# Backward row pairs, per-head global keys and an earlier hand-over of PSUM banks in a fused attention, Fourier mixing and FFN kernel

## The chip, the cores and the metric

The kernel runs on one core of one Trainium2 chip. The metric is the device time of one execution in microseconds (us); lower is better. TensorE is called PE, its weight loads PEld, VectorE DVE, ScalarE ACT, GpSimd POOL and SyncE SP.

## The reference

Attention over 768 positions in 4 batches and 8 heads of 64, with a local window of 96, 8 global keys and a linear bias by distance; then a two-dimensional Fourier transform of the attention's result (its real part is added to it), a normalisation, and an FFN with ReLU of width 2048:

```python
def _attn_ref(q, k, v, n_global, n_local):
    scores = scale * np.matmul(q, k.transpose(0, 1, 3, 2))
    is_global = pos[None, :] < int(n_global)                 # 8
    is_local = (rel >= 0) & (rel < int(n_local))             # 96
    dist = np.where(is_global & ~is_local, float(n_local), np.abs(rel))
    scores = scores - slopes[:, None, None] * dist
    scores = np.where(is_global | is_local, scores, -1e9)
    a = softmax(scores)
    return np.matmul(a, v)

def _moe_ref(x, w_ch1, w_ch2):
    mixed = np.real(np.fft.fft(np.fft.fft(x, axis=1), axis=2))
    u = x + mixed
    un = (u - mean(u)) / np.sqrt(var(u) + 1e-6)
    return u + np.maximum(un @ w_ch1, 0.0) @ w_ch2
```

Here `x` is the attention's result, [4, 768, 512]. q, k, v, the FFN's two matrices and the result are float32 in HBM; the products are made in float16.

## The kernel before, in words

A batch's work is done by head pairs (`hp`, four of them). A pair's q and k are loaded as float16, transposed into `qkT` (`trans`: on PE for batches 0 and 1, by a transposing DMA on SP for batches 2 and 3), multiplied in three groups of 128-row tiles (`score`; in batches 0 and 1 the bias is added by products of `sid` and `dist`), and exponentiated on ACT into `ex`. The global keys are treated apart. `kg_copies` picks the first eight keys of each head into `kG`, `glob` multiplies them with q into a [64, 512] tile whose rows are (pair, head, key), one exp on ACT makes `EG` from it, and `v_global` picks the eight value rows with a selection matrix `sel` on PE; their copies in PSUM go to `vG` on ACT or DVE. `ones` makes the column of ones in `vG` in the same way at the start. `av` multiplies `ex` with the values and adds the global part, 130 columns for both heads of a pair in one product. A norm on DVE divides into `x`.

The Fourier part folds `x` on DVE (`fold_0`, `fold_s`, `fold_d`), multiplies the folded parts with a table of cosines and sines along the positions (`y_unit`, four groups), and multiplies the results with a second table along the features (`u_unit`). The 768 positions are 6m + r with m = 0 to 127 and r = 0 to 5; rows are the six values of r, and PAIRS says which two are made together: (1, 2), (0, 3), (4, 5). Since the transform of a real input is symmetric, not all of its parts are multiplied: rows 4 and 5 are read from parts of rows 2 and 1 that POOL has reversed (`mirror`, line 962). In batch 0 `x` is added on PE by products with a 0-1 matrix (`spread`, line 993); in the others `x` is written to HBM (`bounce`, `xd`), read back in the order of rows (`xr`), and added on DVE (line 1039).

`nt_unit` transposes the normalised rows, `ph_unit` makes the FFN's first products (eight groups for each pair of rows, counted by c = 3b + pair), `pg_unit` the second ones, and the last four row pairs use a form with fewer products (`pg_units`, `pgA` and `pgD`). Stores to HBM go by SP.

The order of each engine's instructions is made before the program runs: a planner (class `Plan`) keeps a clock for every engine, takes from four lists (MIX, ATT, PH, PG, looking ten units ahead in the first two) what it thinks can start first, and corrects these times by a table BIAS. Its costs (`act`, `dve`, `pl.pe(...)`, `dma=`) are estimates written in the code. PSUM has eight banks: ring `xx` has two slots of two banks, `C` and `D` are two banks each for the attention of the first batches, and are given back together (token `("CD",)`), when all their users are done, as the rings `ph` and `pg`. Every buffer is counted, so a unit waits until the buffer that it overwrites is free.

Loads with a cast go by POOL's software queue, in the order in which they're listed. At the start SP loads the first pair's q and k as float32 (they're cast on ACT or DVE), then `ident`, `dist` and `gb`; meanwhile PE runs 12 products of zeros (`pz`, line 1384).

Of the kernel before, what the change touches and what calls it, by code (L numbers as in the profile page):

```python
# [9 lines left out]
FP16 = mybir.dt.float16  # L10
# [12 lines left out]
class Plan:  # L23
# [8 lines left out]
    LAND = {}  # L32
    LAT = {"ACT": 0.14, "DVE": 0.12, "POOL": 0.08}

    def __init__(self):
        self.t = {"PE": 0.0, "ACT": 0.0, "DVE": 0.0, "POOL": 0.0, "SP": 0.7, "DMA": 3.75, "DMA2": 1.9}
        self.tok = {}
        self.ready = []
        self.pending = []
        self.rings = {}  # L40
        self.left = {}
        self.n = 0
        self.lanes = [0.0] * 8
        self.soft = [0.0] * 8
# [64 lines left out]
    def emit(self, place):  # L109
# [8 lines left out]
        if dma:  # L118
            q = "DMA2" if outs and outs[0] in (("ld", 0), ("ld", 1), ("c", "id"), ("c", "dist"), ("c", "gb")) else "DMA"
            end = self.t[q] = max(self.t[q], end) + dma  # L120
        else:
            lat += self.LAT.get(eng, 0.0)
# [26 lines left out]
    def slot(self, tag):  # L149
# [7 lines left out]
    BIAS = {('mk1', '*', 4): 1.5, ('y', 1, 2, 2, 'r'): -3, ('qk', '*', 2): -0.7, (2, 90): -0.7, ('ob', '*', 2): -0.3,  # L157
            (3, '*', 7): -1.5, ('ex', 2, 2, 0): 1.5, ('ss', '*', 6): 0.3, (0, 20): -3, (1, 57): -0.7, ('mk1', '*', 5): 1.5,
            ('v', '*', 1): 1.5, ('c', 't2'): -0.3, ('mk1', '*', 7): 0.7, ('kG', '*', 1): 0.7, ('z', 1, 0): 3, ('u', 2, 0): 0.7}
# [4 lines left out]
    AQ = (4, 5)  # L164
    ORD = {("qk", 0): 0, ("v", 0): 0, ("qk", 1): 5, "w1": 6, "gate": 7, ("v", 1): 8, "w2": 9, ("qk", 2): 10, ("v", 2): 10, ("qk", 3): 10, ("v", 3): 10}

    def run(self, streams):

        left = [[(*u, (i, k)) for k, u in enumerate(s)] for i, (s, _) in enumerate(streams)]
        while True:  # L170
            best = None
            for i, s in enumerate(left):
                for k, (needs, ring, _, name) in enumerate(s[:self.LOOK if streams[i][1] else 1]):
# [3 lines left out]
                    if ring is not None:  # L177

                        there = [(min(self.rings[g])[0], g) for g in ring
                                 if self.rings[g] and not (g in ("C", "D") and ("CD",) in self.tok)]  # L180
# [27 lines left out]
def act(n):  # L208
    return 0.06 + n / 1200.0


def dve(n):
    return 0.085 + n / 960.0
# [11 lines left out]
def kernel(  # L225
# [63 lines left out]
    sel = np.zeros((P, 128))  # L289
    gpos = np.flatnonzero(tau < NG)  # L290
    for h in range(4):
        for g in range(NG):
            sel[gpos[g], h * 32 + h * NG + g] = 1.0
    gb = np.zeros((64, 1))
    for h in range(H):
        at = 32 * (h // 2 % 2) + 16 * (h // 4) + 8 * (h % 2)
        gb[at:at + NG, 0] = -slopes[h] * NL
    perm = np.zeros((P, 9, 64))
    for rho in range(3):
        for jj in range(3):  # L300
            for m in range(64):
                y = 3 * m + rho - 64 * jj
                if 0 <= y < 64:
                    perm[y, 3 * rho + jj, m] = perm[64 + y, 3 * rho + jj, m] = 1.0
    ident_sel = np.concatenate([np.eye(P), sel], 1)
# [20 lines left out]
    early = {"ctx": tc.tile_pool(name="pse", bufs=1, space=bass.MemoryType.PSUM)}  # L326
    early["pool"] = early["ctx"].__enter__()

    def bank(tag, name, dtype=FP32):
        if tag in ("C", "D"):  # L330
            return early["pool"].tile([P, 2, 512 if dtype == FP32 else 1024], dtype, tag=tag, name=name, bufs=1)
        if tag == "xx":
            return ps.tile([P, 2, 512 if dtype == FP32 else 1024], dtype, tag=f"{tag}{tag.k}", name=name, bufs=1)
        if "late" not in early:
            early["ctx"].__exit__(None, None, None)
            early["late"] = ctx.enter_context(tc.tile_pool(name="psl", bufs=1, space=bass.MemoryType.PSUM))
        return early["late"].tile([P, 512], FP32, tag=f"{tag}{tag.k}", name=name, bufs=1)

# [12 lines left out]
    ident = kon.tile([P, 256], FP16, tag="ident", name="ident")  # L351
    sel_sb = ident[:, 128:256]
# [4 lines left out]
    gb_sb = kon.tile([64, 1], FP32, tag="gb", name="gb")  # L357
# [7 lines left out]
    one = kon.tile([P, 1], FP16, tag="one", name="one")  # L365
# [3 lines left out]
    vG = [kon.tile([P, H, 66], FP16, tag=f"vG{i}", name=f"vG{i}") for i in range(2)]  # L369

    EG = kon.tile([P, 512], FP16, tag="eg", name="eg")
# [32 lines left out]
    def load_qk(b, hp):  # L404
# [3 lines left out]
        for w, src in enumerate((q, k)):  # L408
# [14 lines left out]
            if n == 0:  # L423
                def read(w=w, rows=rows):
                    t = stage["u", w] = buf("u", w, [P, 2 * NP, 2 * Dh], FP32, 1)
                    nc.sync.dma_start(t, rows)
                pl.later([("SP", 0.45, read)], [], 0.0, [("ld", w)], lat=1.7, dma=1.35)

                def cast(on, w=w):
                    place()  # L430
                    copy_on(on, qk16[n][:, w].rearrange("p h n t d -> p (h n) (t d)"), stage["u", w])
                pl.later([("ACT", act(768), lambda cast=cast: cast("ACT")), ("DVE", dve(768), lambda cast=cast: cast("DVE"))], [("ld", w)], 0.0,
                         [("qk", 0, w)], [("free", "u", w)], rank=0)
# [19 lines left out]
    pl.users(("CD",), 4 * HP + 4 + HP + len(YG) + NP + 1)  # L453

    def BANKS(b):
        return ("xx", "C", "D") if b < pl.CDB else ("xx",)

    def CD(b, ring):
        if b == 1 and ring in ("C", "D"):
            pl.left[("CD",)][0] += 1  # L460
            return [("CD",)]
        return [("CD",)] if b == 0 else []
# [5 lines left out]
    def kg_copies(b, hp):  # L468
        n = HP * b + hp
        for s in range(2):  # L470
            def cp(on, s=s):
                c0 = 16 * (hp // 2) + 8 * s
                on.tensor_copy(  # L473
                    kG[b % 2][64 * s:64 * s + 64, hp, c0:c0 + NG].rearrange("p (t m) -> p t m", t=2),
                    TT[n][64 * s:64 * s + 64, 1, 0:P].rearrange("p (t m) -> p t m", t=2)[:, :, 0:NG // 2])
            pl.later([("POOL", 0.2, lambda cp=cp: cp(nc.gpsimd))] + [("DVE", 0.12, lambda cp=cp: cp(V))] * (b == 0), [("qkT", n)] + ([("gldone", b - 2, hp % 2)] if b > 1 else []), 0.0,
# [1082 lines left out]
```

## Time and profile before

| | us |
|---|---|
| runs (median of 3, lowest, highest) | 262.46, 262.13, 262.70 |
| the profiled execution | 262.43 |
| its span, first to last instruction | 260.5 |
| busy: PE, PEld, DVE, ACT, POOL | 246.3, 178.8, 163.1, 142.9, 120.6 |
| FFN: ph (768 products), pg (256 products) | 93.3, 61.1 |
| spread L993 (36), second transform L1017 (192 in three forms) | 4.6, 8.5 + 4.4 + 2.2 |
| av L685 (352), with the global part L677 (64) | 16.9, 12.6 |
| first transposition, first ph | starts at 8.29, 50.62 |
| end of the last product, end of the span | 257.1, 260.5 |

A busy time is the time in which at least one instruction of the group was under way; PE's instructions overlap, so the mean duration of one is longer than the distance between two. Times within the profile count from the span's start. The granted clock of PE is given in tenths of full speed by slice; over the span it is 0.993.

### The profile page before, as it was taken

Reading aid. Unit: us, or ns where it says so; the run is one execution under the profiler, and the core shown is the slowest. Engines: PE = TensorE matmul, PEld = TensorE weight load, DVE = VectorE, ACT = ScalarE, POOL = GpSimd, SP = SyncE. Lnnn points to the kernel's source line nnn. Section 1 sums busy time; section 2 is a strip of 40 time slices with the busy share of each in tenths; the row PEclk is TensorE's granted clock in tenths of the full one; section 3 lists DMA queues with packets and bytes.
Section 4 is the critical chain, followed back from the end, with each engine's and each line's share of the span. In section 5 each row is a group of like instructions: output and inputs, shape, how many; then the busy total and the mean of one; then the engine's idle time right before and its main releaser. Section 6 shows DMA issues by size and latency. Waiting matters only on the chain.

```text
span 260.5 us, 6774 instructions
## 1 busy us (share of the span) xinstructions
PE 246.3 (95%) x2824; PEld 178.8 (69%) x2824; DVE 163.1 (63%) x362; ACT 142.9 (55%) x240; POOL 120.6 (46%) x212
## 2 busy tenths in 40 slices
PE   7798789899979999999999999999999999999994
PEld 2566545589748676575477466588779578888883
DVE  1549996537982746712277987778996555625463
ACT  4198798685636698851055743884645236533300
POOL 8798876724938988999921304030304011010000
PEclk9799999999999999999999999999999999999999
DMA  7999999997999999999968941401450540300222
GB/s 175 174 165 179 274 207 108 90 194 102 138 159 218 158 138 149 140 112 123 114 126 167 178 182 48 115 3 43 108 178 0 83 121 0 93 30 3 81 83 81
DMA packets 93630, 31.52 MB, mean 121 GB/s; under 512 B 81664, under 2 KB 89984, under 8 KB 93600
## 3 DMA queue, kind: packets, MB, share of 16 engines
q0 software_dynamic: 66096, 14.18, 62.5%
q1 hardware_dynamic: 24672, 12.19, 21.2%
q10 hardware_dynamic: 2832, 4.72, 6.9%
q8 instruction: 22, 0.36, 0.6%
q14 instruction: 8, 0.07, 0.1%
HBM read 30.95 MB, written 8.65 MB: 152 GB/s over the span
## 4 chain that ended last, share of the span: by engine, by line
PE 55%; POOL 19%; DMA 17%; ACT 3%; DVE 3%; issue 2%; ACTq 0%; POOLq 0%
PE ph L1144 18%; PE pg L1168 12%; POOL qk L414 10%; DMA v<-in_v_dram 7%; DMA qk<-in_q_dram 6%; PE pgD L1249 5%; POOL v L400 5%; DMA w<-in_moe_w_ch_dram 4%; PE pgA L1249 4%; PE pav L685 3%; PE py L914 3%; PE pu L1017 2%; PE pt L507 1%; DVE x L704 1%; POOL hT L438 1%
## 5 line engine op out<-in xcount | busy, mean ns | idle before, releaser
L1144 PE MATMUL ph<-unT,w 128*128 128x256 f16 x768 | 93.3, 273 | 2.9 <-ACT hT L1150 1.7
L1144 PEld LDWEIGHTS <-w 128*128 128x128 f16 x768 | 73.1, 98 | 16.1 <-issue 4.9
L1150 ACT ACTIVATE hT<-ph 128x512 f16<-128x512 f32 x83 | 48.9, 596 | 47.6 <-PE ph L1144 47.3
L1168 PE MATMUL pg<-w,hT 128*128 128x512 f16 x256 | 61.1, 379 | 0.0
L1168 PEld LDWEIGHTS <-hT 128*128 128x128 f16 x256 | 24.1, 98 | 23.8 <-issue 1.2
L1089 POOL TENSOR_SCALAR sm<-sm 128x2 f32<-128x2 f32 x12 | 3.0, 254 | 57.4 <-ACT un L1082 57.2
L400 POOL DMA_DIRECT2D v<-in_v_dram x32 | 24.7, 823 | 0.7 <-DMA hT<-in_k_dram 0.7
L583 ACT ACTIVATE ex<-sc 128x992 f16<-128x992 f32 (+2 forms) x24 | 20.6, 928 | 7.1 <-DVE qkT L514 5.6
L580 ACT ACTIVATE er<-sc 128x768 f16<-128x768 f32 (+2 forms) x24 | 21.6, 925 | 4.5 <-PE sc L555 3.3
L414 POOL DMA_DIRECT2D qk<-in_k_dram x32 | 21.4, 750 | 4.6 <-DMA qk<-in_k_dram 3.1
L1177 DVE SCALAR_TENSOR_TENSOR u<-pg,sm,u 128x512 f32<-128x512 f32 x16 | 12.0, 750 | 18.0 <-PE pg L1168 18.0
L414 POOL DMA_DIRECT2D qk<-in_q_dram x32 | 21.4, 730 | 3.4 <-DMA qk<-in_q_dram 2.0
L1073 ACT ACTIVATE un<-u,sm 128x512 f16<-128x512 f32 x17 | 11.8, 717 | 19.1 <-DVE sm L1043 17.6
L962 POOL COPY ww<-zy 128x512 f16<-128x512 f16 x16 | 10.1, 661 | 21.4 <-PE py L914 14.4
L595 DVE TENSOR_TENSOR ex<-er,mk 128x768 f16<-128x768 f16 (+2 forms) x24 | 15.4, 662 | 4.2 <-ACT er L580 4.2
L1082 ACT ACTIVATE un<-un 128x512 f16<-128x512 f16 x24 | 14.9, 625 | 4.5 <-DMA unT<-un 4.5
L1039 DVE SCALAR_TENSOR_TENSOR u<-pu,xr 128x512 f32<-128x512 f32 x18 | 11.7, 688 | 9.0 <-PE pu L1017 9.0
L685 PE MATMUL pav<-v,ex 128*128 128x65 f16 x352 | 16.9, 193 | 0.0
L473 POOL COPY kG<-qkT 64x8 f16<-64x8 f16 x28 | 9.6, 342 | 15.7 <-DMA qkT<-qk 12.8
L685 PEld LDWEIGHTS <-ex 128*128 128x128 f16 x352 | 15.6, 97 | 0.8 <-issue 0.2
L1151 DVE TENSOR_SCALAR hT<-ph 128x512 f16<-128x512 f32 x13 | 9.0, 690 | 8.3 <-PE ph L1144 8.3
L931 DVE CAST zy<-py 128x512 f16<-128x512 f32 (+1 forms) x8 | 7.1, 892 | 10.4 <-PE py L914 8.2
(143 smaller groups left out, 388.6 us busy)
## 6 DMA issues: line engine op xcount, KB each, us to landing
out_dram<-u SPq DMA_DIRECT2D x23, 256.0 KB, 2.1
w<-in_moe_w_ch_dram POOLq DMA_DIRECT2D x8, 512.0 KB, 11.0
v<-in_v_dram POOLq DMA_DIRECT2D x32, 96.0 KB, 6.5
xr<-xd ACTq DMA_DIRECT2D x3, 768.0 KB, 4.7
qk<-in_q_dram POOLq DMA_DIRECT2D x32, 48.0 KB, 4.0
qk<-in_k_dram POOLq DMA_DIRECT2D x32, 48.0 KB, 3.7
xd<-x ACTq DMA_DIRECT2D x4, 384.0 KB, 4.6
hT<-in_q_dram POOLq DMA_DIRECT2D x5, 192.0 KB, 7.4
```

The costliest lines, as they stand in the source:

```text
L400: nc.gpsimd.dma_start(v16[b % 2][64 * t:64 * t + 64, h0:h0 + 2, :, 0:Dh].rearrange("m h i d -> m (h i) d"), v[b, h0:h0 + 2].rearrange("h ( ...
L414: nc.gpsimd.dma_start(qk16[n][64 * t:64 * t + 64, w, :, h], src[b, h0 + h].rearrange("(i m t) d -> t m i d", m=64, t=2)[t])
L580: A(mine(), cut(pa), AF.Exp, 0.0, 0.125)
L583: A(cut(expst[hp][:, :, g * 512:g * 512 + (384 if g == 2 else 512)]), cut(pa), AF.Exp, 0.0, 0.125)
L595: VT(o, mine(), m, op=ALU.mult)
L685: nc.tensor.matmul(o[:, s * 65:(s + 1) * 65], lhsT, v16[b % 2][:, 2 * hp + s, i, 0:65], start=(j < 2 and a == 0), stop=(a == len(ops) - 1) ...
L1082: A(x, x, AF.Square, accum_out=MV[c][:, a, 2:3])
L1144: nc.tensor.matmul(ph[:, a * CH:(a + 1) * CH].rearrange("p (x m) -> p x m", x=2), W1[0][:, d, jb * P:(jb + 1) * P], UNT[c][:, :, d, :], st ...
L1150: pl.later([("ACT", act(512), lambda: A(dst, ph, AF.Relu)), ("DVE", dve(512), lambda: V.tensor_scalar_max(dst, ph, 0.0))], [], e, [("h", c ...
L1168: nc.tensor.matmul(pg, HT[c][:, jb, t * P:(t + 1) * P], W2[0][:, jb, :], start=(jb == 0), stop=(jb == NJ - 1))
L1177: V.scalar_tensor_tensor(UT[c][:, t, :], pg, MV[c][:, t, 3:4], UT[c][:, t, :], op0=ALU.mult, op1=ALU.add)
L1249: nc.tensor.matmul(o, lhs(j), rhs(j), start=(first and j == 0), stop=(j == NK - 1), skip_group_check=True)
```

## The change

The parts, as the code does them:

1. `ident` is loaded first on SP, then the first pair's q; its k and `dist` are loaded by ACT. q is cast on DVE, k on ACT. 18 instead of 12 products of zeros.
2. Batch 0's order is pair 0's scores, pair 2's transposition, the global keys of pairs 0 and 2, pair 1's transposition, pair 2's scores, av of pair 0, and so on. Before the first score group of each batch-0 pair, four products of `ident` with `dist` are put into the same bank and overwritten.
3. Global keys: each pair has its own 32 rows (eight keys used, the rest with a bias of -30000), each head its own half of `EG`; glob's products use one head's 64 rows each, two exps take the place of one. The value rows come from HBM by 16 small SP loads and are copied on ACT or DVE. `sel`, `ones` and `v_global`'s products are gone. av's global part is two products of 65 columns.
4. Rows 4 and 5 are rows 2 and 1 backwards: in batches 1 to 3 the same bank of rows 1, 2 is evacuated a second time in reverse (`back`), and rows 4 and 5 have no products of their own; partition p then holds m = 127 - p, so `xr`'s rows 4, 5 are gathered and the result is scattered by indirect DMA on POOL, with a list of row numbers `back_sb`. In batch 0 the products are made, from unreversed parts, with the spread reversed. `mirror` keeps only its first copy. PAIRS is (1, 2), (4, 5), (0, 3).
5. spread reads `x` in its own order and writes PSUM with a step.
6. Banks C and D have tokens of their own: C goes to `ph`, D to `pg`. y groups 2, 3 and the later u units of batch 0 use only `xx` and `D`. The units of rows 1, 2 come after y groups 0 and 1.
7. The read-back of `xd` is issued by SP.
8. The planner's costs, landing times and BIAS are other numbers.

```diff
-    LAND = {}
+    LAND = {("c", "id"): 3.0, ("ld", 0): 4.8, ("ld", 1): 5.0, ("c", "dist"): 6.3, ("c", "gb"): 6.5}
...
+    BIAS = {('h', 7, 2): 1.5, ('g0', '*', 1): 1.5, ('ss', '*', 7): 1.5, ('rd', '*', 10): -0.3, ('u', 3, 0): 1.5, (1, 19): 0.3,
...
+    HW = (0,)
+    U0 = 2
+    PZ = 18
+    FILL = 4
+    EARLY = ("qk2", "qk1", "v0", "v2", "qk3", "v1", "v3")
...
+                    (nc.scalar if w else nc.sync).dma_start(t, rows)
...
+            for _ in range(pl.FILL if b == 0 and g == 0 else 0):
+                nc.tensor.matmul(pa[:, 0, :], idn, dist_sb[:, 0, 0:512], start=True, stop=True, skip_group_check=True)
...
-            e = pl.pe(0.25 + 0.21 * pem, start, True)
+            e = pl.pe(0.27 + 0.28 * pem, start, True)
...
+    def v_global(b):
+        for hp in range(HP):
+            r = slice(32 * HQ[hp], 32 * HQ[hp] + NG)
+            def ld(hp=hp, r=r):
+                nc.sync.dma_start(vgs[r], v[b, 2 * hp:2 * hp + 2, 0:NG, :].rearrange("h g d -> g h d"))
+            def cp(on, hp=hp, r=r):
+                dst = vG[b % len(vG)][r, hp, :, 0:Dh]
...
+            for n in ns:
+                for s in range(2):
+                    r, o = slice(64 * s, 64 * s + 64), 32 * HQ[n % HP]
+                    nc.tensor.matmul(pg[o:o + 32, s, :], kG[b % 2][r, n % HP, :],
+                                     TT[n][r, 0, 256:S], start=True, stop=True, tile_position=(64 * s, o))
...
+                for s in range(2):
+                    A(EG[rows, s], pg[rows, s, :], AF.Exp, gb_sb[rows, s:s + 1], 0.125)
...
-                        nc.tensor.matmul(o.rearrange("p (h d) -> p h d", d=65), EG[:, (j - 2) * P:(j - 1) * P], vG[b % 2][:, 2 * hp:2 * hp + 2, 0:65],
-                                         start=True, stop=False, skip_group_check=True)
                     for s in range(2):
+                        if j >= 2:
+                            nc.tensor.matmul(o[:, s * 65:(s + 1) * 65], EG[:, s, (j - 2) * P:(j - 1) * P], vG[b % len(vG)][:, hp, s, 0:65],
+                                             start=True, stop=False, skip_group_check=True)
...
-            eng.dma_start(XR[b], rows)
+            nc.sync.dma_start(XR[b][:, 0:4], rows[:, 0:4])
+        def rg():
+            nc.gpsimd.indirect_dma_start(out=XR[b][:, 4:6].rearrange("p r d -> p (r d)"), out_offset=None,
+                                         in_=XD[b].rearrange("(n r) d -> n (r d)", r=2),
+                                         in_offset=bass.IndirectOffsetOnAxis(ap=back_sb[:, 0:1], axis=0))
...
-    PAIRS = ((1, 2), (0, 3), (4, 5))
+    PAIRS = ((1, 2), (4, 5), (0, 3))
...
-                        nc.tensor.matmul(pu[64 * h:64 * h + 64, a, :].rearrange("p (r n) -> p r n", r=4), PX[0][t, 3 * (r // 2) + jj],
-                                         X[0][t, 3 * h + jj].rearrange("p (n r) -> p r n", r=4), start=(jj == 0), stop=False,
+                        hx = 1 - h if pr == 1 else h
+                        nc.tensor.matmul(pu[64 * h:64 * h + 64, a, :].rearrange("p (r n) -> p n r", r=4), PX[0][t, 3 * (r // 2) + jj],
+                                         X[0][t, 3 * hx + jj].rearrange("p (n r) -> p n r", r=4), start=(jj == 0), stop=False,
...
+                evac(c, pu, ring, e, pr)
+                if pr == 0:
+                    evac(c + 1, pu, ring, e, 1)
...
+        def back():
+            fresh(c)
+            u, sm = UT[c], MV[c]
             for a in range(2):
+                o, x = (t[:, i].rearrange("p (n r) -> p r n", r=4) for t, i in ((u, a), (XR[b], 4 + a)))
+                i = pu[:, 1 - a, ::-1].rearrange("p (r n) -> p r n", r=4)
+                V.scalar_tensor_tensor(o[:, 1:4], i[:, 0:3], 1.0, x[:, 1:4],
+                                       op0=ALU.mult, op1=ALU.add, accum_out=sm[:, a, 0:1])
+                V.scalar_tensor_tensor(o[:, 0, 1:P], i[:, 3, 0:P - 1], 1.0, x[:, 0, 1:P],
+                                       op0=ALU.mult, op1=ALU.add, accum_out=sm[:, a, 4:5])
+                V.tensor_tensor(u[:, a, 0:1], pu[:, 1 - a, 0:1], XR[b][:, 4 + a, 0:1], op=ALU.add)
...
-        needs = [("unT", c), ("w1", jp // 2)] + (free("hT", 4 + c) if jp == 0 else []) + [("CD",)]
+        needs = [("unT", c), ("w1", jp // 2)] + (free("hT", 4 + c) if jp == 0 else []) + [("C",)]
...
+    def store_back(c, needs):
+        b = c // NP
+        def st():
+            nc.gpsimd.indirect_dma_start(out=out.rearrange("b (n r) d -> (b n) (r d)", r=2),
+                                         out_offset=bass.IndirectOffsetOnAxis(ap=back_sb[:, b:b + 1], axis=0),
+                                         in_=UT[c].rearrange("p r d -> p (r d)"), in_offset=None)
...
-        needs = [("h", c, 2 * part), ("h", c, 2 * part + 1), ("w2", part)]
+        needs = [("h", c, 2 * part), ("h", c, 2 * part + 1), ("w2", part), ("D",)]
```

## The prediction

> **What bounds the kernel now.** I read the page first: engines' busy time, then the span in slices.
>
> ```profile
> span 260.5 us, 6774 instructions
> ...
> PE 246.3 (95%) x2824; PEld 178.8 (69%) x2824; DVE 163.1 (63%) x362; ACT 142.9 (55%) x240; POOL 120.6 (46%) x212
> ...
> PE   7798789899979999999999999999999999999994
> ...
> PEclk9799999999999999999999999999999999999999
> ```
>
> TensorE is the bound, and the page has no other engine near it. From slice 13 on it stands at 9. What can be gained is either less TensorE work, or the holes of the first 12 slices. So next the table by stage, cut where the first transposition, the first FFN product and the last product stand.
>
> ```profile
> 0.00:8.30 8.30, 5.01 (x22) 1.77 (x22) 1.36 (x12) 2.97 (x3) 7.26 (x17) 1.00 0.88 179
> 8.30:50.60 42.30, 37.10 (x745) 24.99 (x741) 32.10 (x102) 32.02 (x47) 33.24 (x55) 0.96 1.59 170
> 50.60:128.00 77.40, 75.29 (x797) 53.36 (x798) 39.97 (x76) 46.72 (x83) 60.00 (x97) 1.00 1.52 149
> 128.00:200.00 72.00, 71.80 (x777) 51.85 (x774) 57.77 (x117) 41.66 (x70) 16.03 (x37) 1.00 0.46 105
> 200.00:257.10 57.10, 57.07 (x496) 46.87 (x494) 31.37 (x59) 19.55 (x38) 4.05 (x11) 1.00 0.21 58
> ```
>
> The columns are stage, length, busy PE, PEld, DVE, ACT, POOL, clock, DMA. A busy PE isn't a PE at its pace, so I priced each stage's products by the spacing of their starts in the timeline where they run packed: ph 0.109 us (8 in 0.87), pg 0.2155, pu L1017 0.056 (16 in 0.89), av 0.030 for 65 columns and 0.056 for 130, a batch-0 or -1 score group some 0.4, twelve L993 products 1.46. The four stages from 8.3 hold 31.6, 72.7, 70.0 and 56.5 us of work in 42.3, 77.4, 72.0 and 57.1 us. Lost: 10.7, 4.7, 2.0 and 0.6. Two thirds of the loss lies before the first FFN product. The start, from the timeline of PE:
>
> ```profile
> 1.17 4.80 PE L1384 MATMUL pz<-eg 128*128 128x512 f16 x12 [1.17 <-DVE eg L1379]
> 8.10 0.27 PE L1423 MATMUL pones<-one,ident 128*32 128x1 f16 x8 [2.12 <-DMA ident<-idm]
> 8.29 2.87 PE L507 MATMUL pt<-ident,hT 128*64 128x128 f16 x48
> ...
> 17.91 0.86 PE L507 MATMUL pt<-ident,hT 128*64 128x128 f16 x24
> ```
>
> The warm-up ends at 5.97, PE idles until ident lands, and the 48 transpositions then take 2.87 us where 24 later take 0.86: the clock of 5 to 15 us is granted at 0.88 and 0.78. The one long hole later is told by the timeline of all engines:
>
> ```profile
> 75.74 0.35 ACTq L732 DMA_DIRECT2D xr<-xd  x1
> 76.14 0.74 ACT L1407 ACTIVATE mk<-distk 128x640 f16<-128x640 f16 x1 [4.01 <-DMA xd<-hT]
> ...
> 77.41 1.91 PE L1144 MATMUL ph<-unT,w 128*128 128x256 f16 x16 [1.74 <-ACT hT L1150]
> ```
>
> ScalarE's queue stood 4.0 us at the read-back of xd, waiting for the write; the ReLU behind it came late, and PE idled 1.74 us.
>
> **The change part by part.** The sum is against the profiled execution, 262.43 us (span 260.5 and 1.9 around it); the median of the runs is 262.46.
>
> *First pair and warm-up: -1.1.* Before, q landed about 3.96 and k about 5.77 (the casts L443 start there), ident at 8.1. Ident now leaves first on SP, k on ScalarE. Even if q and k land no earlier than 5.8, the two casts of 0.84 lie side by side and end by 6.6. The warm-up of 18 products ends later: the first ten step by 0.43 us, to about 5.5, the other eight by 0.2155, so 7.2. Transpositions start at 7.2 instead of 8.3. The six products more cost nothing while the casts last, and 0.6 beyond.
>
> *The clock of the first products: -1.8.* 48 transpositions at the later pace are 1.7 instead of 2.87, and the six following blocks of scores lose some 0.6 less. Four filler products before each batch-0 pair's first scores are 4 x 4 x 0.2155 = 3.4 us. They run while VectorE copies qkT (0.96 us, L514), which the scores need. For the first pair all four are covered; for the others partly. If no cover were left they would cost 3.4, with full cover nothing; I charge 1.4.
>
> *The rest of the stage 8.3 to 50.6: -2.5.* The order is now pair 0's scores before pair 2's transposition, and av of pair 0 before pair 1's scores. ScalarE's first exp came at 12.18; from 7.2 it is 0.9 transposition, 1.0 copy, 0.3 scores: 9.4. VectorE sat idle 2.24 us before 18.81, then ran full to 39.3: its first norm can now lie some 4 us earlier, in that idle time. But ScalarE has two eg exps more of 0.68 in batch 0, and pair 3's load still comes by the same gpsimd queue (pt at 17.91), so I count 2 us of the 3 to 4, not all. Products for rows 1, 2 now follow y groups 0 and 1 with no reversed copy, and ph needs only bank C: the first ph, at 50.6 before, comes near 44, and ph products fill holes that attention left. After clock and start the stage had 8.9 us of loss; I take 4 of it away and charge those 1.4 of filler, rounding -2.6 to -2.5 and not charging the filler twice.
>
> *Row pairs 4, 5 in batches 1 to 3: -2.7.* 48 products of L1017 at 0.056 go. POOL loses L962 (10.1 us) and half its kG copies (9.6). VectorE's backwards evacuation: two of 384 at 0.55 (0.687 less 128 columns of 1.05 ns, the slope between L1267's 256 and 512), two of 127 at 0.28, accumulator reads of 0.08, five small ones of some 0.16: 2.8 instead of 1.7, so +1.1 three times. VectorE is at 63%; this is covered as long as the PSUM slot isn't wanted. It is held 4.5 us instead of 1.7. I charge 0.5 in all.
>
> *Global keys: -1.1.* 32 value selections (0.03 each) and eight ones-products go, 1.2. Their eight copies give way to sixteen of 128 columns on eight partitions (0.2 to 0.25) behind small SP loads. 64 av products of 130 columns become 128 of 65: two times 0.030 against 0.056, +0.3. The 16 glob products become 32 on half the rows; pairs of these can overlap. If they don't, +3.4; if four overlap as L559's four tiles do, -1; I take -0.2. ScalarE gets five more exps of 0.68, three of them in stages with 40% idle.
>
> *Read-back moved to SP: -1.7.* The 4.0 us wait is then SP's. Behind it stand batch 2's transpositions by DMA, issued from 78.3 and used for scores after 94: covered. In batches 1 to 3 rows 4, 5 of xr come by a gather on POOL, 0.75 to 0.85 us by the nearest rows (L400, L414), after xr has landed at 80.4, 152 and 195; 4 us later they are there, by 84.5, 156.5 and 199.5. The first evacuations ran at 86.35, 158.76 and 200.01. Two fit, the third fits because rows 1, 2 go first. Four scattered stores replace eight SP stores; POOL's loads wait behind one of them until its rows are ready.
>
> [...] No row of this trace has an indirect transfer. [...]
>
> *The spread L993: 0, with both ends kept.* Twelve now take 1.46 with a strided moving operand, against 0.65 for three rounds of four tiles. The change reads contiguously and writes PSUM in strides. [...] The trace has no strided PSUM write, so I leave the row's time.
>
> Sum: -1.1 -1.8 -2.5 -2.7 +0.5 -1.1 -1.7 = -10.4. The new order of everything else, which the planner derives from changed costs and biases, isn't seen; later stages hold 7.3 us of loss, 1.7 already spent, so it can give little and can cost. I charge 1. 262.4 - 9.4 = **253.0 us**.
>
> **The rivals.** *(a) Half of it, 256 to 260, chance 0.20.* Batch 0 is held by loads: av waits for v (a wait at 15.9 shows it), pair 3 lands at 17.9 whatever was done at the start, and fillers and the two exps take what is freed. Then only the 7 or so us of removed work and stall, less the order's costs, remain: 257. For it: ScalarE is full from 12.2 to 20, VectorE from 19 to 39. Against it: their first idle ends 3 us sooner.
>
> *(b) Slower, 266, chance 0.15.* [...]
>
> *(c) The steps do as told, 249 to 256, chance 0.62.* *(d) Nothing to see, 0.03*: filler and order cancel it.
>
> **How the numbers follow.** The likeliest is (c), 253.0. 248.5 is this with the spread's gain of 2.4 and an order that costs nothing and hides the filler. Upwards the range takes all of (a) and, to 261.5, the part of it where glob does not overlap or the spread is slower, leaving out (b) and a few in 100 below. A difference under 0.2% (0.5 us) can't be told from none. Faster: (c), (a): 0.82; same 0.03; slower 0.15.
>
> **What would show it.** First transposition near 7.2 at full clock; first ph near 44; no wait of ScalarE for xd; POOL's indirect DMAs near 1 us; 144 instead of 192 L1017 products; L993's twelve near 1.5; VectorE's backwards part near 2.8. Wrong would be PE holes behind pu's slot, POOL busy above 130 us, or the stage from the first ph on longer than its work by more than the present 7 us.

## The result, and the profile after

The change makes the kernel 0.7% faster: the ratio to the kernel before, measured side by side, is **0.9931 [0.9903, 0.9959]**, about 1.8 us of 262.8. Medians of all twenty runs are 261.34 us after (258.81 to 266.68) and 262.76 us before. The forecast was 253.0, so the direction held, at the upper end of the range, and the size was a fifth of it.

The profiled execution of the changed kernel took 264.43 us and is one of four slow ones that the ratio leaves out, so the profile of the experiment e7 stands beside it: the same kernel but for the queue that issues one kind of transfer, with a span of 258.2 us and a full clock (1.00) in every window that is read here.

The page of the changed kernel:

```profile
span 262.7 us, 6833 instructions
...
PE 246.2 (94%) x2838; PEld 177.1 (67%) x2838; DVE 165.4 (63%) x399; ACT 145.0 (55%) x243; POOL 116.0 (44%) x185
...
PE   7888989999999999997995899999999999999994
...
PEclk9999999999999999999999599999999999999999
```

A slice is 6.57 us. Up to slice 6 (39 us) the digits sum to 48 tenths against 46 before, and a part of these is filler; slices 7 to 12, now all at 9, have gained. The clock is now full in every slice up to there. A new hole stands at slice 22 (138 to 145 us), and in the next one the clock falls to half. The stages, cut at the first transposition, the first ph and the last product, with the columns of the table of before (length, PE, PEld, DVE, ACT, POOL, clock, DMA):

```profile
0.00:6.80 6.80, 5.35 (x20) 2.04 (x20) 3.38 (x25) 2.12 (x2) 6.19 (x14) 1.00 0.79 191
6.80:49.60 42.80, 37.66 (x793) 25.39 (x792) 30.48 (x95) 33.77 (x48) 29.50 (x44) 1.00 1.67 181
49.60:128.00 78.40, 75.97 (x797) 52.97 (x784) 41.96 (x94) 48.90 (x89) 62.77 (x100) 1.00 1.49 145
128.00:200.00 72.00, 67.99 (x732) 47.45 (x731) 55.38 (x118) 36.99 (x63) 10.09 (x16) 0.95 0.50 102
200.00:259.30 59.30, 59.28 (x520) 49.26 (x518) 33.71 (x69) 23.20 (x44) 7.42 (x13) 1.00 0.19 57
```

The stage up to the first ph was to shrink from 42.3 to about 37 us. It is 42.8 us long. Pricing the products again by the spacing of their starts (one set of prices for all three kernels, so that the figures for before differ by up to 0.6 from the prediction's), work and lost time in us are:

| stage | before: work, lost | changed, as profiled | changed, e7's profile |
|---|---|---|---|
| first transposition to first ph | 31.2, 11.2 | 34.3, 8.6 | 34.4, 7.8 |
| first ph to 128 | 72.9, 4.5 | 73.3, 5.1 | 72.2, 5.7 |
| 128 to 200 | 69.7, 2.3 | 63.6, 8.4 | 69.3, 2.7 |
| 200 to the last product | 56.7, 0.4 | 58.9, 0.4 | 54.5, 0.3 |

In the first row the lost time did fall by about 3 us, and the work rose by as much: 16 filler products of 0.2155 are 3.4 us. TensorE's holes were filled with filler. The third row shows what this one execution lost beyond e7's, 5.7 us; no part of the account below rests on it. PE's timeline of the changed kernel:

```profile
1.45 5.40 PE L1428 MATMUL pz<-eg 128*128 128x512 f16 x18 [1.45 <-DVE eg L1423]
6.78 0.86 PE L527 MATMUL pt<-ident,hT 128*64 128x128 f16 x24
7.57 1.04 PE L555 MATMUL sc<-dist,ident 128*128 128x512 f16 x4
...
38.81 1.03 PE L933 MATMUL py<-t,ww 128*128 128x256 f16 x8
...
49.66 0.50 PE L1178 MATMUL ph<-unT,w 128*128 128x256 f16 x3
...
124.23 0.28 PE L1023 MATMUL pu<-t,rev 128*128 128x128 f16 x2 [1.81 <-POOL rev L969]
126.12 0.40 PE L650 MATMUL pgl<-qkT,kG 64*32 64x512 f16 x6 [0.62 <-POOL kG L494]
145.25 0.59 PE L577 MATMUL sc<-qkT 64*128 64x256 f16 x4 [3.92 <-DMA qkT<-qk]
```

The abbreviations are the kernel's names: pt transpositions, sc scores, py and pu the two steps of the Fourier part, pgl the global keys. The first transposition is at 6.78 (8.29 before) and the first 24 take 0.86, the full pace. But y starts at 38.81 (before 38.99), and the first ph at 49.66 (before 50.62). 1.5 us won at the start are 0.2 us thirty microseconds later. Then come three waits, for POOL's reversed copy, for its kG copy, and for the transposing DMAs of batch 3; for the same things the kernel before waits 0.2 us at most. In e7 they are 1.7, 0.6 and 1.2 us.

### The profile page after: what moved, and what is told of

It reads as the page before. It is cut to its first block, busy times and chain, and to the rows that moved or that the text cites. A ratio compares the mean times of both kernels' runs of the same rounds, so it can differ in the third digit from the quotient of the medians.

```text
span 262.7 us, 6833 instructions
## 1 busy us (share of the span) xinstructions
PE 246.2 (94%) x2838; PEld 177.1 (67%) x2838; DVE 165.4 (63%) x399; ACT 145.0 (55%) x243; POOL 116.0 (44%) x185
## 4 chain that ended last, share of the span: by engine, by line
PE 51%; DMA 18%; POOL 18%; ACT 5%; issue 3%; SPq 1%; DVE 1%; POOLq 0%; ACTq 0%
PE ph L1178 18%; PE pg L1211 11%; POOL qk L433 10%; DMA qk<-in_k_dram 8%; PE pgD L1295 5%; DMA w<-in_moe_w_ch_dram 5%; PE pgA L1295 4%; POOL v L419 4%; DMA hT<-in_k_dram 3%; DMA qkT<-qk 3%; PE py L933 2%; ACT ex L605 2%; PE pav L695 2%; SPq L505 1%; PE pu L1023 1%
## 5 line engine op out<-in xcount | busy, mean ns | idle before, releaser
L1184 ACT ACTIVATE hT<-ph 128x512 f16<-128x512 f32 x85 | 50.2, 597 | 54.5 <-PE ph L1178 54.1
L1211 PEld LDWEIGHTS <-hT 128*128 128x128 f16 x256 | 24.4, 98 | 24.7 <-issue 1.7
L602 ACT ACTIVATE er<-sc 128x992 f16<-128x992 f32 (+2 forms) x24 | 21.7, 924 | 9.5 <-PE sc L577 6.3
L419 POOL DMA_DIRECT2D v<-in_v_dram x32 | 26.0, 863 | 0.9 <-DMA hT<-in_k_dram 0.6
L433 POOL DMA_DIRECT2D qk<-in_q_dram x32 | 22.1, 778 | 3.3 <-DMA qk<-in_k_dram 2.3
L617 DVE TENSOR_TENSOR ex<-er,mk 128x992 f16<-128x992 f16 (+2 forms) x24 | 14.8, 629 | 13.4 <-ACT er L602 13.2
L433 POOL DMA_DIRECT2D qk<-in_k_dram x32 | 22.2, 825 | 0.9 <-DMA v<-in_v_dram 0.9
L1195 POOL DMA_INDIRECT out_dram<-u,back x4 | 4.6, 1142 | 39.3 <-DVE u L1313 21.0
L1108 ACT ACTIVATE un<-u,sm 128x512 f16<-128x512 f32 x12 | 8.6, 721 | 12.1 <-DVE sm L1090 7.4
L688 PE MATMUL pav<-vG,eg 128*128 128x65 f16 x128 | 14.3, 193 | 0.9 <-DVE x L714 0.9
L948 ACT ACTIVATE zy<-py 128x1024 f16<-128x1024 f32 (+1 forms) x14 | 11.3, 841 | 6.1 <-PE py L933 5.6
L1295 PEld LDWEIGHTS <-hT 128*128 128x128 f16 x128 | 12.5, 98 | 1.8
L714 DVE TENSOR_TENSOR x<-pav,rc 128x384 f16<-128x384 f32 x24 | 12.6, 554 | 0.6
```

The source lines that it names most:

```text
L419: nc.gpsimd.dma_start(v16[b % 2][64 * t:64 * t + 64, h0:h0 + 2, :, 0:Dh].rearrange("m h i d -> m (h i) d"), v[b, h0:h0 + 2].rearrange("h ( ...
L433: nc.gpsimd.dma_start(qk16[n][64 * t:64 * t + 64, w, :, h], src[b, h0 + h].rearrange("(i m t) d -> t m i d", m=64, t=2)[t])
L602: A(mine(), cut(pa), AF.Exp, 0.0, 0.125)
L617: VT(o, mine(), m, op=ALU.mult)
L688: nc.tensor.matmul(o[:, s * 65:(s + 1) * 65], EG[:, s, (j - 2) * P:(j - 1) * P], vG[b % len(vG)][:, hp, s, 0:65], start=True, stop=False, ...
L1184: pl.later([("ACT", act(512), lambda: A(dst, ph, AF.Relu)), ("DVE", dve(512), lambda: V.tensor_scalar_max(dst, ph, 0.0))], [], e, [("h", c ...
```

## The experiments

**e1, no fillers.** `FILL = 0` in place of 4.

> The sixteen filler products are left out; order and all else are as after the change. Theory A (the stage before the first FFN product is held by VectorE, ScalarE and the loads, and the fillers fill holes of PE): no change within 0.3%, first ph within 0.5 us of 49.7. Rival (the fillers are work that the stage pays for, since three of the four pairs' keys lie transposed before): the ratio to the kernel before falls by 0.006 to 0.013, first ph 2 to 3.5 us earlier. If the fillers hold the clock up, the granted clock between 7 and 20 us falls instead and the time rises by 1 us or more.

Measured: ratio 0.9813 [0.9758, 0.9869], which does not overlap the interval of the changed kernel. The difference of 0.0118 is 3.1 us; both intervals together leave 1.5 to 4.7. PE's timeline without fillers:

```profile
6.92 0.86 PE L527 MATMUL pt<-ident,hT 128*64 128x128 f16 x24
...
8.83 0.41 PE L581 MATMUL sc<-qkT 64*64 64x256 f16 x8 [0.72 <-DVE qkT L534]
...
37.40 1.03 PE L933 MATMUL py<-t,ww 128*128 128x256 f16 x8
...
48.25 1.92 PE L1178 MATMUL ph<-unT,w 128*128 128x256 f16 x16
```

The cover that the prediction named is there: PE waits 0.72 us for the qkT copy when no filler stands in it. Four fillers last 0.96 us (7.57 to 8.54 in the timeline of the changed kernel), so the four groups are work of 3.4 to 3.8 us. Yet y and the first ph come only 1.4 us earlier without them (1.8 against e7's first ph). About half of the filler was covered, and loads are a part of the cover: in e1 PE waits 2.7 us for later q and k loads between 11 and 26 us, 1.05 in the changed kernel's profile and not at all in e7's. What e1 won beyond 1.4 us lies behind the first ph and isn't located. The clock is full without the fillers too (1.00 over the 257.0 us of this profile), so they bought nothing that shows.

**e10, the start alone.** The kernel before, with the changed start and every other instruction in its old order (the old load of `ident`, which comes later on SP, is left out):

```diff
                 def read(w=w, rows=rows):
                     t = stage["u", w] = buf("u", w, [P, 2 * NP, 2 * Dh], FP32, 1)
-                    nc.sync.dma_start(t, rows)
+                    if w == 0:
+                        nc.sync.dma_start(ident, id_d.ap())
+                    (nc.scalar if w else nc.sync).dma_start(t, rows)
...
-                    copy_on(on, qk16[n][:, w]...
+                    copy_on("ACT" if w else "DVE", qk16[n][:, w]...
...
-        for _ in range(12):
+        for _ in range(18):
             nc.tensor.matmul(pz[:, 0, :], EG[:, 0:P], EG, start=True, stop=True)
```

> The kernel before with the start of the changed one and nothing else: ident first on SyncE, k on ScalarE's queue, q cast on VectorE and k on ScalarE, 18 products of zeros; the order of all other work as before. Forecast's first two steps (start -1.1, clock of the first products -1.8): first transposition near 7.0, ratio 0.989. Rival (the head start is lost before the first ph, since VectorE is full to 39 us and pair 3's loads and the values come when they come): first transposition near 7.0 too, but y within 0.6 us of 39.0, first ph within 0.6 us of 50.6, ratio 0.998 to 1.002.

Measured: ratio 0.9985 [0.9951, 1.0018]. In the profiled execution 14 of the 18 products of zeros stepped at half pace (0.43 us), against 6 in the changed kernel's (6.96 us in all against 5.40), so the first transposition was at 8.26 and not at 7.0, a miss of both expectations. The transpositions were at full pace from there, however (36 in 1.20 us, 12 in 0.53, as in e1 at a clock of 1.00), and ScalarE's first exp started at 10.93 instead of 12.18. PE's timeline in e10:

```profile
8.26 1.20 PE L509 MATMUL pt<-ident,hT 128*64 128x128 f16 x36
9.80 0.53 PE L509 MATMUL pt<-ident,hT 128*64 128x128 f16 x12 [0.35 <-DMA hT<-in_k_dram]
...
16.88 0.53 PE L509 MATMUL pt<-ident,hT 128*64 128x128 f16 x12
18.23 0.53 PE L509 MATMUL pt<-ident,hT 128*64 128x128 f16 x12 [0.82 <-DMA hT<-in_k_dram]
...
39.00 2.31 PE L916 MATMUL py<-t,ww 128*128 128x256 f16 x18
```

The lead of 1.25 us ends at one line: the transposition of the last pair's k, which waits for its load. VectorE's copy behind it, from the timeline of VectorE, first of the kernel before and then of e10:

```profile
18.81 0.96 DVE L514 COPY qkT<-pt 128x1536 f16<-128x1536 f16 x1 [2.24 <-PE pt L507]
```

```profile
18.80 0.96 DVE L516 COPY qkT<-pt 128x1536 f16<-128x1536 f16 x1 [3.25 <-PE pt L509]
```

Same instant, and VectorE has waited 1.01 us longer for it. From there on it has work to 39 us without a pause worth naming, and y starts at 39.00 against 38.99. In the old order a lead of 1.25 us is worth nothing; it turns into idle time of VectorE.

The new order can be asked the same, since its profiles differ in when the zeros end (6 to 12 slow steps) and hardly in anything else before the first ph:

| profile | fillers | first transposition | y | first ph |
|---|---|---|---|---|
| changed kernel | yes | 6.78 | 38.81 | 49.66 |
| e7 | yes | 7.97 | 39.24 | 50.09 |
| e1 | no | 6.92 | 37.40 | 48.25 |
| e5 | no | 7.98 | 37.57 | 48.43 |

1.2 us at the first transposition are 0.4 at the first ph with fillers, and 1.1 us are 0.2 without. The chain of work that leads up to y (each piece followed back to what released it) shows why in e1: it holds two loads of k by POOL's queue and reaches 22.94 us on them.

```profile
4.05 7.57 DMA hT<-in_k_dram
...
14.93 8.01 DMA hT<-in_k_dram
```

In e7, which starts later, the chain holds all four groups of fillers and none of these loads.

**e9, pair 3 earlier.** Without fillers, and without one planner bias, so that the first scores of pair 3 come near 20 us instead of 27.9:

```diff
-    BIAS = {..., ('u', 3, 0): 1.5, (1, 19): 0.3,
+    BIAS = {..., ('u', 3, 0): 1.5,
...
-    FILL = 4
+    FILL = 0
```

> The changed kernel without its filler products and without the planner's bias of +0.3 on one unit, the first score group of pair 3 in batch 0 (it then comes before the transpositions of batch 1's first pairs; the planner also orders much behind it anew). Theory (pair 3's late scores hold batch 0: its values, the last part of VectorE's fold and so y wait for them): pair 3's first scores near 20 us instead of 27.9, y about 2 us earlier than without the fillers alone (37.4, so near 35.5), first ph near 46, ratio to the kernel before about 0.973. Rival (VectorE's own full row of work from 20 to 39 us sets y, in whatever order the pairs come): y within 0.6 us of 37.4, first ph within 1 us of 48.3, ratio 0.981 as without the fillers.

Measured: ratio 1.0267 [1.023, 1.0304], which no theory expected. y started at 37.78 and the first ph at 48.63, so for batch 0 the rival's numbers were right: y doesn't come earlier with pair 3's first scores. Its reason, a full row of VectorE, isn't shown by this. What made it slower lies far behind, at 150 to 200 us, where the planner, from a slightly different state, chose another order. The list of PE's waits, and the window 155 to 160 of this run:

```profile
PE py L933 <- ACT er L602: 4.3, 1, 4.3
PE pgl L650 <- DVE u L1087: 2.1, 1, 2.1
```

```profile
155.00:160.00 5.00, 0.65 (x7) 0.49 (x4) 4.03 (x10) 1.38 (x2) 0.00 (x0) 0.62 0.14 52
```

TensorE works 0.65 of these 5 us. One bias of 0.3 in a table of over a hundred moves the time by 4.5% (1.0267 against 0.9813), over six times the whole effect of the change.

**e2, POOL's small copies given to VectorE.** The kG copies of batches 1 and 2 and `mirror`'s copies of batches 1 to 3, at the same places of the order:

```diff
-        pl.later([("POOL", 0.25, lambda: cp(nc.gpsimd))] ...
+        pl.later([("POOL", 0.25, lambda: cp(V if b in (1, 2) else nc.gpsimd))] ...
...
-            nc.gpsimd.tensor_copy(rev[:, 0, :, 0:1], src[:, 0, :, 0:1])
+            on = V if b else nc.gpsimd
+            on.tensor_copy(rev[:, 0, :, 0:1], src[:, 0, :, 0:1])
```

> The copies of global keys of batches 1 and 2, and the reversed copy of batches 1 to 3, are given to VectorE at the same places of the program; the order of the other instructions stays. Theory B (these small POOL copies stand behind the loads of batches 2 and 3 in POOL's queue, come near 124 us, and hold PE's u product of rows 0, 3, the global products of batch 2 and through them batch 3's transposing DMAs): PE's waits of 1.8 and 0.6 us near 123 to 126 go, batch 3's transposing DMAs start 1 to 3 us before 127, ratio 0.006 to 0.015 lower than the change's 0.993. Rival (the loads themselves are late, the copies only stand beside): the wait moves to the scores of batch 3 and the ratio moves by less than 0.003.

Measured: ratio 0.9878 [0.9833, 0.9923], lower than the changed kernel's but with an interval that overlaps it. It stands on five of twelve times (257.37 to 260.61); six lie from 261.27 to 264.00, and one at 631.77. The wait for `rev` is gone, and the next in line takes its place, from the list of PE's waits:

```profile
PE pgl L650 <- DVE kG L494: 1.7, 1, 1.7
```

Why POOL is late there, from its timeline in the changed kernel:

```profile
120.28 2.00 POOL L419 DMA_DIRECT2D v<-in_v_dram  x2
122.58 1.06 POOL L1195 DMA_INDIRECT out_dram<-u,back  x1 [0.30 <-issue]
123.64 0.21 POOL L968 COPY rev<-zy 128x2 f16<-128x2 f16 x1
123.76 0.41 POOL L969 COPY rev<-zy 128x254 f16<-128x254 f16 x1
124.11 0.40 POOL L970 COPY rev<-zy 128x256 f16<-128x256 f16 x1
124.44 0.22 POOL L494 COPY kG<-qkT 128x32 f16<-128x32 f16 x1
```

The copies stand behind the last loads of batch 3 and the first scattered store, one after the other. This change took from POOL the reversals of L962 (10.1 us) and more than half of its kG copies (9.6 to 4.3 us), and it is still the engine that TensorE waits for: loads, 0.78 to 0.86 us each (the means of L433 and L419), stand in front of these copies up to 122.28, and the scattered store, which the change added, up to 123.64.

**e3 and e4, one batch's value loads left out.** In e3 the changed kernel, in e4 the kernel before, without the eight loads of batch 3's values; batch 3 then uses those of batch 1.

```diff
             def run(t=t):
+                if b == 3:
+                    return
                 nc.gpsimd.dma_start(v16[b % 2]...
```

> Batch 3's eight value loads are left out (batch 1's values are used again), so POOL's queue of loads is some 7 us shorter; all else as after the change. Theory B with its second part (the gain of the start is lost since POOL's loads end near 126 us as before): POOL's loads end near 119, PE's waits between 120 and 146 us fall by 4 us or more, ratio 0.975 to 0.983. Rival (PE is the bound all through and the waits are those of single disturbed executions): ratio within 0.003 of 0.993.

> The same loads are left out of the kernel before the change. Theory B (before, PE had work enough at that place): ratio 0.996 to 1.001. Rival (fewer loads help every order alike): ratio 0.975 to 0.99, as much as in the changed kernel.

Measured: e4 0.9991 [0.995, 1.0032], no change; POOL's loads do not hold the kernel before. e3 gives no ratio (median 263.35, with times from 257.39 to 264.67). Its profile, of an execution of 262.11 us, answers the question in part. The loads in front of the copies ended at 117.33 instead of 122.28, but POOL then stood 3.64 us at the scattered store, and the reversed copy came only 1.6 us sooner. From POOL's timeline in e3:

```profile
120.96 1.06 POOL L1197 DMA_INDIRECT out_dram<-u,back  x1 [3.64 <-DMA out_dram<-u]
122.02 0.22 POOL L970 COPY rev<-zy 128x2 f16<-128x2 f16 x1
```

The scattered store waits for an earlier store of SP to land (POOL's 3.64 us), and SP's next store waits for the scattered one (8.2 us in e7, below). PE's wait for `rev` is gone, as in e2, and PE still waited for batch 3's transposing DMAs. From PE's and from SP's timeline in e3:

```profile
144.00 0.40 PE L579 MATMUL sc<-qkT 64*128 64x256 f16 x4 [4.45 <-DMA qkT<-qk]
```

```profile
125.50 16.14 SPq L507 DMA_TRANSPOSE qkT<-qk  x8
```

So the end of the loads alone isn't what makes these scores late. The eight transposing DMAs take 16 us and stand in SP's queue behind that next store. The changed order has this wait in e7's profile too; from the list of SP's waits there:

```profile
SPq L1225 <- DMA out_dram<-u,back: 8.2, 1, 8.2
```

In e7 the scattered store is issued at 123.55 and the first transposing DMA starts at 128.09, 0.56 us after the store that had waited; in the changed kernel's profile the three stand at 122.58, 127.12 and 0.56, with the same 8.2 us of SP. So one operation that the change added holds both POOL's copies and SP's transposing DMAs. No run takes it away, so what it costs isn't shown.

**e5, e1 and e2 together.**

> The fillers are left out and the small copies of the second experiment are on VectorE. If the two costs are separate (fillers in the first 50 us, copies behind POOL's loads near 124 us), their gains add: 0.981 and 0.988 against the change's 0.993 make 0.976, within 0.005. If PE only waits later for the same transposing DMAs of batch 3, the second gain is lost and the ratio stays at 0.981.

Measured: no ratio. Two of six times are 257.4 and 258.0, the others 262.4 to 264.1. Inconclusive: it isn't shown that the two gains add. The lowest time, 257.38, is that of e2, 257.37, which has the fillers.

**e6 and e8, batch 3's transposing DMAs pair by pair.** q and k of one pair next to each other, instead of four q and then four k; e6 on the changed kernel, e8 on e5's.

```diff
-        for w in range(2):
+        if b == 3:
+            pl.later([("SP", 3.6, lambda: (xb(0), xb(1)))], ...)
+        for w in range(2 * (b < 3)):
```

> In the changed kernel batch 3's transposing DMAs are issued pair by pair, q then k, instead of q of all pairs and then k; the planner knows them as one step of 3.6 us, so the order from 127 us on is new. Theory C (the wait of 3.9 us at 141 to 145 is for the seventh of eight transposing DMAs of some 2 us, which PE's order takes to be there earlier): the wait for qkT falls below 1 us, the granted clock of that stretch stays at 1.0, and the ratio falls by 0.006 to 0.016 to 0.977 to 0.987. Rival (the wait belongs to disturbed executions only): within 0.003 of 0.993.

> All three edits: no fillers, small copies on VectorE, batch 3's transposing DMAs pair by pair. If the three costs are separate places, the ratio is 0.965 to 0.973; if the copies and the pairs cure the same wait, 0.972 to 0.978, no better than the fifth experiment.

Measured: e6 1.001 [0.9964, 1.0056], e8 0.9918 [0.9877, 0.9958]. The wait for the transposing DMAs is gone from both profiles. e6 lies above the changed kernel, with intervals that don't overlap; e8's base e5 has no ratio, and e8 lies above e1. PE's waits in e6 (an execution of 267.28 us, the median is 265.62):

```profile
PE pu L1026 <- POOL rev L972: 3.7, 1, 3.7
PE sc L580 <- DVE u L1074: 2.1, 1, 2.1
```

The planner made a new order again, with new holes. Removing one late arrival by changing what the planner knows doesn't test that arrival alone; e6 and e8 show only that in these two orders nothing was won with it.

**e7, the read-back on ScalarE's queue again.** `nc.scalar.dma_start(XR[b][:, 0:4], ...)` in place of `nc.sync`, at the same place of the order.

> The read-back of rows 0 to 3 is issued by ScalarE again, at the same place of the program; all else as after the change. If the step was worth what the prediction counted, ScalarE waits some 4 us for xd near 68 to 72, a ReLU comes late, and the ratio rises by 0.005 to 0.008. Rival (PE had enough other work there): within 0.002 of 0.993.

Measured: ratio 0.9864 [0.9801, 0.9926]; below what both expectations named, and not slower than the changed kernel (the intervals overlap). ScalarE's timeline in e7:

```profile
72.03 0.33 ACTq L742 DMA_DIRECT2D xr<-xd  x1
72.41 0.74 ACT L1451 ACTIVATE mk<-distk 128x640 f16<-128x640 f16 x1 [1.38 <-issue]
```

In the new order the read-back is placed when the write of xd is almost done, and holds the queue for 1.38 us at most, while TensorE is fed. The 4.0 us stall before was a matter of where the instruction stood, not of the queue that issued it.

**e11, the saved products put back twice.** Without fillers, the 16 products of rows 1, 2 are made three times in each of batches 1 to 3:

```diff
-                for x in range(2):
+                for x in (0, 1) * (3 if b and pr == 0 else 1):
                     nc.tensor.matmul(o, yy[:, x, :], t2_sb[:, rd, ...
```

> The changed kernel without fillers in which the 16 products of rows 1, 2 of the batches 1 to 3 are made three times over: 96 more products of the kind of which the change took 48 away. Forecast's step (48 such products are worth 2.7 us, TensorE being the bound where they stood): 5.4 us more than without the fillers alone, ratio 0.9813 + 0.0205 = 1.002. Rival (they lie in holes that TensorE has there anyway, waits for POOL's copies and the transposing DMAs): under 2 us more, ratio below 0.989.

Measured: ratio 1.0017 [0.9976, 1.0059], against 0.9813 in e1. The difference, 0.0204, is 5.4 us for 96 products, 0.056 us each, just the price taken. Both intervals together leave 3.5 to 7.2 us. In the two profiles the span grew by 2.1 us only (257.0 to 259.1), while PE's wait for `rev` at 124 fell from 2.1 to 0.4 us: a part of the added work fell into that wait. So products added there cost about their time, less what a wait behind them takes back; that those taken away were worth as much is concluded from this.

## Why the prediction was wrong in size

The step that failed is what the sum did with the stage up to the first ph: it counted the start (-1.1), the clock (-1.8) and the rest of the stage (-2.5) in full at its end, 5.4 us. The first ph came 1.0 us earlier (49.66), 0.5 in e7 (50.09), and 2.2 to 2.4 without fillers (48.43 and 48.25).

**Start (-1.1) and clock (-1.8): true where they stand, wrong in the sum.** The clock is 1.00 from the first transposition to 128 us, and 24 transpositions take 0.86. The first transposition at 6.78 against 7.2 foretold is in part luck: the forecast took ten slow products of zeros from one profile, and the ten profiles with the new order show 6 to 12 of them and transpositions from 6.78 to 8.06. At the end of the stage the lead is worth nothing in the old order (e10: 18.80 against 18.81) and 0.2 to 0.4 us of 1.1 to 1.2 in the new one (the table under e10). It ends at loads of POOL's queue, which come when they come. Rival (a) had named the last pair's load, and was weighed at 0.20.

**Rest of the stage (-2.5): failed, and so did the first ph near 44.** The text had not carried its own sum over: 50.6 less 5.4 is 45.2. And of the 4 us of loss that it takes away, it prices only 2. The step counted VectorE's idle 2.24 us before 18.81 as time to be moved. In the changed kernel VectorE still waits in several places; from its timeline:

```profile
10.72 0.96 DVE L534 COPY qkT<-pt 128x1536 f16<-128x1536 f16 x1 [1.86 <-PE pt L527]
...
15.87 0.20 DVE L712 RECIPROCAL rc<-pav 128x6 f32<-128x6 f32 x1 [1.86 <-PE pav L695]
```

The waits of the kernel before between 9 and 39 us (0.62, 1.11, 0.72, 2.24 and 0.18) are 4.9 us, those of the changed kernel (1.86, 0.92, 1.86, 0.80, 0.63, 0.23 and 0.27) 6.6. The first norm came 3.9 us earlier, at 15.87 instead of 19.81, just as the step said; the end of VectorE's row stayed at 39 us. So VectorE's row isn't the bound by itself. Without fillers the chain to y runs over the loads (e1), with them over the fillers (e7), and y moves by 1.4 to 1.8 us between the two: several arrivals lie close together, and taking one away shows the next. This is rival (a)'s mechanism, with its words on fillers. Which of them each microsecond belongs to isn't settled.

**The filler (1.4, inside that sum): right at the first ph.** It costs 1.4 us there (1.8 against e7). e1's ratio says 3.1, with 1.5 to 4.7 left open.

**Row pairs 4, 5 (-2.7, +0.5): the products were sized right, the evacuation wasn't.** 144 products of L1023 are left, and e11 gives 0.056 us for one added (0.036 to 0.075 by its intervals). The backward evacuation is dearer than 2.8 us a batch. From the groups of VectorE:

```profile
L1083 DVE SCALAR_TENSOR_TENSOR u<-pu,xr 128x384 f32<-128x384 f32 x6 | 5.1, 846 | 3.9 <-DMA out_dram<-u 3.9
L1085 DVE SCALAR_TENSOR_TENSOR u<-pu,xr 128x127 f32<-128x127 f32 x6 | 2.3, 381 | 0.0
```

384 elements read backwards with a step take 0.846, where 512 forwards take 0.684 (L1071). With accumulator reads and small instructions (the lines from L1083 to L1090) it is some 3.9 us a batch. In the changed kernel's and e7's profiles PE doesn't wait for it; in e9 it does, 2.1 us for L1087, a line of this evacuation.

**Global keys (-1.1): about as foretold, not tested alone.** Eight glob products now step in 0.35 (166.49 to the next start at 166.84 in e7) where four took 0.55 (165.87 to 166.42 before); the four tiles overlap, the better end of the bounds. With the 1.2 of value selections and ones gone and 0.3 added in av, it comes to about 1.7 us of TensorE's work.

**Read-back (-1.7): the stall went, but not by this edit.** e7 has the old queue back and no such stall.

**Order (+1): too little.** The waits for POOL's copies and the transposing DMAs are 3.5 us in e7's profile (1.7, 0.6, 1.2); the kernel before has none above 0.2. The prediction's own sign of being wrong came: behind the first ph TensorE lost 8.7 us in e7, and 7.2 before. The scattered store has a part in it, as a release and not by its 1.06 us (e3); the rest is where the planner put things, which is argued and not shown. e9 shows how far order alone reaches.

**Gather and scatter: near 1 us, as foretold.** From POOL's groups:

```profile
L1195 POOL DMA_INDIRECT out_dram<-u,back x4 | 4.6, 1142 | 39.3 <-DVE u L1313 21.0 <-DVE u L1220 18.0 <-issue 0.3
L745 POOL DMA_INDIRECT xr<-xd,back x3 | 3.3, 1098 | 10.9 <-DMA xd<-x 10.3 <-issue 0.3 <-DMA out_dram<-u 0.2
```

The means are 1.14 and 1.10 us. No run shows the slowdown to 266 that rival (b) gives 0.15: with these transfers the median is 261.34. The waits behind the bars, 10.9 and 39.3 us, are POOL standing until the data is there. The prediction had this too, that what comes behind a scattered store waits; it named POOL's loads, and the record shows the small copies.

**Spread (0): right.** Twelve products that write PSUM in strides take 1.48 (from PE's timeline at 33.33), before 1.52 to 1.53 in the same view with strides in what they read. The slower spread that the range allows for is in no run, nor is the gain of 2.4 us, which counts 0.65 for the twelve. Whether the stride in PSUM prevents that gain isn't shown, since no run has neither stride.

Together, from e7's profile, whose last product ends at 254.8 against 257.1: up to the first ph 0.5 us came of 5.4. Behind it TensorE's work fell by 3.3 us (199.3 to 196.0 in the table) of 3.8 foretold (2.7 and 1.1), and its lost time rose by 1.5 (7.2 to 8.7), where -1.7 for the stall, +0.5 for the bank and +1 for the order make -0.2. So 4.9 of the 7.1 us that are missing there are the failed step. Which single placement of the planner makes the rest isn't settled: e2, e3, e5, e6 and e8 each moved one, and got another in its place or no verdict. A smaller slip changes nothing: of the 18.0 us lost before, 10.7 are three fifths and not two thirds. The version without fillers has the lowest ratio that was measured, below both kernels; the intervals of e7 and e2 overlap its own.

## What to carry to other kernels

A gain at the start of a chain is worth what is left of it at the next arrival that doesn't depend on it: before a head start is put into a sum, look for the first wait on a load behind it, and count up to there. Filler work is free only inside a wait that is at least as long and is still there with the filler in it; look at each place, not at the first. An operation that two queues wait for is priced by what stands behind it in both, not by its own length. Where a planner orders the program from cost estimates, an edit of its numbers is a new program: put a price on order from a trial of a small edit (here 4.5% from one bias of 0.3) before believing a sum of 1 to 3%.

## What the runs showed of the hardware

The granted clock fell to half in a long wait of TensorE and was still there behind it. e9 shows it best, where all six times agree within 0.3%; from PE's timeline, and the windows from 157 us:

```profile
159.48 3.57 PE L933 MATMUL py<-t,ww 128*128 128x256 f16 x16 [4.35 <-ACT er L602]
```

```profile
157.00:160.00 3.00, 0.52 (x3) 0.40 (x3) 2.06 (x6) 1.38 (x2) 0.00 (x0) 0.50 0.08 29
160.00:163.00 3.00, 3.00 (x16) 2.14 (x15) 0.68 (x2) 1.31 (x2) 0.00 (x0) 0.50 0.00 0
163.00:166.00 3.00, 2.06 (x25) 1.60 (x23) 0.74 (x3) 2.44 (x3) 0.86 (x3) 0.99 0.00 0
```

The 16 products take 3.57 us, where 8 of the kind take 1.03 at full clock (at 37.40 in e1). So the wait costs its 4.35 us and some 1.5 more (3.57 less twice 1.03). In the changed kernel's profile the clock was 0.50 from 145 to 151 after the wait of 3.92 us; in e7 the wait for the same transfers was 1.2 us and the clock stayed at 1.00. The length of the wait alone doesn't tell these cases apart: in the kernel before, 2.12 us without work behind the products of zeros were followed by 0.88 (5 to 10 us) and 0.78 (10 to 15 us); in e1 a wait of 2.12 us left the clock at 1.00. What decides between these isn't settled.

The row of the clock doesn't show everything: the kernel before has 1.00 from 0 to 6 us, while ten of its products of zeros step there by 0.43 us, twice the later 0.2155; 14 step so in e10.
